# Attention over a key/value cache on one core: the instruction order of every engine written out in tables

## The chip, the core and the metric

The kernel runs on one core of a Trainium2 chip. The core has five engines with an instruction queue each: the tensor engine (PE in the profile, PEld for its weight loads), VectorE (DVE), ScalarE (ACT), GpSimd (POOL) and SyncE (SP, which issues all loads and stores here). Each works through its own queue in order; engines wait for one another on semaphores. The metric is the device time of one execution in microseconds (us), as the median of several runs.

## What is computed

Eight sequences of 112 queries are projected with `wq` into 32 heads of 192, attend to a cache of 512 keys and values per head, and are projected back with `wo`. All tensors are bf16.

```
B, Sq, D = 8, 112, 640;  H, Sk, Dh = 32, 512, 192
q = (x @ wq).reshape(B, Sq, H, Dh).transpose(0, 2, 1, 3)
scores = einsum("bhqd,bhkd->bhqk", q, k_cache) * Dh ** -0.5
p = softmax(scores)
o = einsum("bhqk,bhkd->bhqd", p, v_cache)
out = o.transpose(0, 2, 1, 3).reshape(B, Sq, H * Dh) @ wo
```

## The kernel before

**The work.** The 32 heads are taken in two halves of 16. A *tile* t (0 to 15) is one half of the heads of one sequence, and a *step* n (0 to 63) is four heads of a tile: n = 4t + s. Each instruction group has a name that the texts use:

- `X c`: transpose 128 rows of x on the tensor engine; `evX` copies the result out of PSUM.
- `KN`, `K`, `V`: loads of the cache. For tiles 0 and 1, K comes as it lies (`KN`), is transposed on the tensor engine (`K t u` in the tables, `KT` in the code) and copied out by `evK`. For the others one transposing load `K t` brings it. `V t 0` and `V t 8` load the values of eight heads each.
- `Qa`, `Qb (m, lp)`: the projection of two heads for two sequences, ten and five matmuls of 224 columns; `evQa`, `evQb` copy it out on ACT. `qc n` (DVE) copies parts of q to other partitions.
- `S n`: scores of a step, as `Sm` (two halves of four matmuls over all 128 rows of the array) and `St` (the rest of the head size, on 64 rows). They use PSUM banks 0 to 3.
- `smax` (DVE) scales scores into `s_sb` with a row minimum, `exp` (ACT) exponentiates and sums, `rc` and `norm` (DVE) divide. Four of each per step; `s_sb` has two places, so a `smax` waits for the `exp` two before it.
- `PT n j`: transposes of P on the tensor engine; `evPT n 0` copies the first half on ACT, `evPT n 1` the second on DVE. For steps 57 to 61 a transposing DMA `TD n` does it.
- `PV n`: P times V, as `PVt` (64 columns of the array) and `PVm`; `evPV` copies to `oT_sb` on ACT.
- `O (u, f, part)`: a part of the product with `wo` (matmuls of 224 columns) for unit u, that is eight heads of two sequences; `oacc u f` (DVE) adds it to `accT`. `O6`, `OL` and `OF` do the same for the last unit and turn the sums round for the output; `oout` (ACT) copies, `OUT` stores.

**The order.** Operations are declared with what they depend on (`Plan.add`), and `Plan.run` walks the list of each engine, waits for what an operation needs, and issues it. Semaphore values follow from the lists. So the lists are the program, and only they decide what stands behind what. A group that fills a PSUM bank waits for the copy that emptied it last (`fill`).

In the kernel before, the lists have three sources. Steps 0 to 8 are written out (`FRONT_PE`, `FRONT_ACT`, `FRONT_DVE`, and `FRONT_SP` for the first 34 loads). Steps 9 to 57 follow one rule, which puts on the tensor engine: the scores of step n, PV of step n-2, Q parts due, an O part, both transposes of step n-1, the rest of O and Q. ACT and DVE have rules of their own:

```
s_pe(n)                                      # scores of n
pv_pe(n - 2)
...                                          # Qa of the step, first part of O
pt_pe(n - 1)
...                                          # second part of O, Qb
act += [("exp", n, 0), ("exp", n, 1)] + [("evPV", n - 2)]
act += [("exp", n, 2)] + a_q + [("exp", n, 3)]
act += [("evPT", n - 1, 0)] + b_q
```

The last six steps are again lists (`TAIL` and two lists for ACT and DVE). The order of loads in the middle comes from a loop: `K t`, `V (t-1) 8`, a piece of a weight if one is due, `V t 0`. Q goes to banks 6 and 7, O to bank 7, PT and PV to banks 4 and 5 in these steps. A load waits on SP for its place to come free, and everything behind it in SP's list waits too: `K t` for the scores of step 4t - 5, `V` for the PV that last read its place, the second half of `wo` for the last O that reads the first.

Of the kernel before, what the change touches and what calls it, by code (L numbers as in the profile page):

```python
# [52 lines left out]
def build_mha_kernel(nc, x, k_cache, v_cache, wq, wo, out):  # L53
# [27 lines left out]
    with ExitStack() as es:  # L81
# [111 lines left out]
        def load_wq(half, lp, n=2):  # L193

            def emit(e):
                c0 = lp * 2 * DH
                g0 = half * HU * DH + c0
                return e.dma_start(wq_sb[:, :, c0:c0 + 2 * n * DH],
                                   wq[:, g0:g0 + 2 * n * DH].rearrange("(dc p) c -> p dc c", p=128))
            add("SP", ("WQ", half, lp), [("Qb", 3, lp + n - 1)] if half else [], emit, f"mWQ{lp}", 16)  # L200
            order["SP"].append(("WQ", half, lp))
            wq_piece.update({(half, lp + i): ("WQ", half, lp) for i in range(n)})

        def load_wo(half, u):
# [5 lines left out]
            old = [("O", 6 + u, 3, 1)] if half else [("KT", 1, HU - 1)]  # L210
# [31 lines left out]
        for b in range(B):  # L242
# [4 lines left out]
        FRONT_SP = [  # L247
            ("X", 0), ("WQ", 0, 0), ("KN", 0, 0, 4), ("WQ", 0, 2), ("KN", 0, 4, 4), ("WQ", 0, 4), ("KN", 0, 8, 8),
            ("WQ", 0, 6), ("V", 0, 0), ("X", 1), ("KN", 1, 0, 8), ("V", 0, 8), ("KN", 1, 8, 8), ("V", 1, 0),
            ("X", 2), ("K", 2, 0), ("V", 1, 8), ("WO", 0, 0), ("V", 2, 0), ("K", 3, 0), ("V", 2, 8), ("WO", 0, 1),  # L250
            ("V", 3, 0), ("K", 4, 0), ("V", 3, 8), ("V", 4, 0), ("K", 5, 0), ("V", 4, 8), ("WQ", 1, 0), ("V", 5, 0),
            ("K", 6, 0), ("V", 5, 8), ("WQ", 1, 2), ("V", 6, 0)]
        assert sorted(order["SP"][:len(FRONT_SP)]) == sorted(FRONT_SP)
        order["SP"][:len(FRONT_SP)] = FRONT_SP

        del order["SP"][-3:]
        order["SP"] += [
            ("TD", 57), ("V", 14, 8), ("TD", 58), ("OUT", 0), ("TD", 59), ("V", 15, 0), ("TD", 60), ("OUT", 1),
            ("TD", 61), ("OUT", 3), ("V", 15, 8), ("OUT", 4), ("OUT", 5), ("OUT", 2), ("OUT", 6), ("OUT", 7)]


        END = NN - 6
        NF = 9

        TAIL = [
            ("S", 58), ("OF", 3, 4), ("OF", 0, 5), ("O", 13, 1, 0, 7), ("O", 13, 1, 1, 7), ("O", 12, 2, 0, 6),
            ("OF", 1, 4), ("O", 12, 2, 1, 6), ("S", 59), ("OF", 2, 7), ("PV", 56, 4), ("O", 12, 3, 0, 6),
            ("O", 12, 3, 1, 6), ("O", 13, 0, 0, 7), ("O", 13, 0, 1, 7), ("S", 60), ("PV", 57, 4), ("O", 13, 3, 0, 7),
            ("O", 13, 3, 1, 7), ("O", 13, 2, 0, 6), ("O", 13, 2, 1, 6), ("PV", 58, 4), ("S", 61), ("PV", 59, 4),
            ("O6", 1, 0, 6), ("S", 62), ("O6", 1, 1, 6), ("O6", 0, 0, 7), ("OF", 5, 5), ("O6", 0, 1, 7),  # L270
            ("O6", 2, 0, 6), ("S", 63), ("PV", 60, 4), ("O6", 2, 1, 6), ("PV", 61, 0), ("OL", 0, 0),
            ("PT", 62, 0, 4), ("PT", 62, 1, 5), ("OL", 1, 0), ("OF", 4, 6), ("PT", 63, 0, 0), ("PV", 62, 4),
            ("PT", 63, 1, 1), ("OL", 0, 1), ("OL", 1, 1), ("PV", 63, 0), ("OL", 2, 0), ("OL", 2, 1), ("OL", 3, 0),
            ("OL", 3, 1), ("OF", 6, 4), ("OF", 7, 1)]
        end_bank = {tok[:-1]: tok[-1] for tok in TAIL if tok[0] not in ("S", "OL")}

# [163 lines left out]
        def transposes(n, j):  # L440
            bank = end_bank.get(("PT", n, j), 4 + j)
# [16 lines left out]
        def values(n):  # L458
# [3 lines left out]
            b0 = end_bank.get(("PV", n), 4)  # L462
# [45 lines left out]
        def o_bank(u, f):  # L508
            return end_bank.get(("O", u, f, 0), 7)
# [18 lines left out]
        def o_acc(u, f):  # L528
# [10 lines left out]
            deps = [("O", u, f, 1)] + ([("XT", B * SQ // 128 - 1)] if u == 0 else [])  # L539
# [13 lines left out]
        def o_six(g, part):  # L553

            def emit(e):
                for k in range(18, KB) if part else range(18):
                    w, o = wo_k(k)
                    for j, m in enumerate(SIX[g]):
                        mm = e.matmul(ps[:, end_bank["O6", g, 0], j * SQ:(j + 1) * SQ], w[:, m * 128:(m + 1) * 128], o[:, 0:SQ],
                                      start=(k == 0 and j == 0), stop=(k == KB - 1), skip_group_check=True)  # L560
                return mm
            add("PE", ("O6", g, part), [("evPV", step_of[NT - 2, 2 + part])], emit)

        def o_six_acc(g):
            m0, n = SIX[g][0], len(SIX[g])

            def emit(e):
                src = ps[:, end_bank["O6", g, 0], 0:n * SQ].rearrange("p (c s) -> p c s", c=n)
# [33 lines left out]
        def o_final(b):  # L602
            bp, bb = divmod(b, 2)
            bank = end_bank["OF", b]
# [14 lines left out]
        q_at = {n: [(1, n)] for n in range(4, 8)}  # L619
        for m in range(2, NM):  # L620
            for lp in range(LP):
                q_at[8 * m - (8 if (m, lp) < (3, 2) else 6) + lp] = [(m, lp)]
        o_at = {9: [(0, 0)], 10: [(0, 1)], 11: [(0, 2), (0, 3)], 13: [(1, 0)], 14: [(1, 1)], 15: [(1, 2), (1, 3)]}
        for u in range(2, 2 * NM - 2):
            for f in range(4):
                if 4 * u + 8 + f < END:
                    o_at[4 * u + 8 + f] = [(u, f)]
        whole = [o for n, os_ in o_at.items() for o in os_ if n not in q_at]
# [56 lines left out]
        def f_pe(b):  # L685
            fill(("OF", b), end_bank["OF", b], ("oout", b))
# [7 lines left out]
        def pt_pe(n):  # L694
            for j in range(2):
                fill(("PT", n, j), 4 + j, ("evPT", n, j))

        def pv_pe(n):
            for j in range(2):
                fill(("PVt", n), end_bank.get(("PV", n), 4) + j, ("evPV", n))  # L700
# [7 lines left out]
        def smaxes(n):  # L708
            return [("smax", n, i) for i in range(4)]

        FRONT_PE = [
            ("X", 1, 6, "DVE"), ("X", 0, 7, "DVE"), ("Z", 10), ("Qb", 0, 0, 3), ("Qa", 0, 1, 2), ("Qa", 0, 0, 4),
            ("K", 0, 1, 5, "ACT"), ("Qb", 0, 1, 3), ("K", 0, 2, 0, "ACT"), ("K", 0, 3, 5, "DVE"),
            ("K", 0, 0, 1, "ACT"), ("Qa", 0, 2, 7), ("S", 0), ("K", 0, 6, 5, "DVE"), ("K", 0, 5, 4, "DVE"),
            ("K", 0, 4, 6, "DVE"), ("Qa", 0, 3, 7), ("K", 0, 7, 0, "ACT"), ("Qb", 0, 3, 1), ("Qb", 0, 2, 7),
            ("Qb", 0, 4, 5), ("S", 1), ("Qa", 0, 5, 4), ("Qa", 0, 4, 7), ("Qb", 0, 5, 1), ("K", 0, 10, 0, "DVE"),
            ("K", 0, 11, 6, "DVE"), ("K", 0, 8, 3, "ACT"), ("K", 0, 9, 2, "ACT"), ("PT", 0, 1), ("Qb", 0, 6, 4),
            ("Qb", 0, 7, 1), ("K", 0, 13, 5, "DVE"), ("Qa", 0, 7, 3), ("PT", 0, 0), ("Qa", 0, 6, 7), ("S", 2),
            ("X", 2, 7, "DVE"), ("PV", 0), ("K", 0, 15, 6, "ACT"), ("X", 3, 0, "DVE"), ("K", 0, 12, 1, "ACT"),
            ("PT", 1, 0), ("PT", 1, 1), ("K", 0, 14, 2, "DVE"), ("Qa", 1, 0, 7), ("S", 3), ("PV", 1),  # L720
            ("Qb", 1, 1, 0), ("K", 1, 1, 7, "DVE"), ("Qa", 1, 1, 1), ("K", 1, 2, 2, "DVE"), ("PT", 2, 0),
            ("PT", 2, 1), ("K", 1, 5, 0, "ACT"), ("K", 1, 3, 6, "DVE"), ("Qa", 1, 3, 3), ("Qb", 1, 0, 5),
            ("K", 1, 0, 1, "ACT"), ("K", 1, 4, 6, "ACT"), ("K", 1, 6, 4, "DVE"), ("K", 1, 7, 5, "ACT"),
            ("Qa", 1, 2, 2), ("Qb", 1, 3, 7), ("S", 4), ("Qb", 1, 2, 6), ("PV", 2), ("K", 1, 10, 0, "DVE"),
            ("Qa", 1, 4, 1), ("Qb", 1, 4, 3), ("K", 1, 9, 2, "DVE"), ("K", 1, 8, 7, "DVE"), ("PT", 3, 0),
            ("PT", 3, 1), ("S", 5), ("PV", 3), ("Qa", 1, 5, 6), ("PT", 4, 0), ("K", 1, 11, 1, "DVE"), ("PT", 4, 1),
            ("K", 1, 12, 7, "ACT"), ("K", 1, 13, 6, "DVE"), ("Qb", 1, 5, 4), ("S", 6), ("PV", 4),
            ("K", 1, 15, 7, "DVE"), ("Qb", 1, 6, 0), ("Qa", 1, 6, 6), ("K", 1, 14, 2, "ACT"), ("PT", 5, 0),
            ("X", 4, 1, "DVE"), ("X", 6, 7, "DVE"), ("PT", 5, 1), ("S", 7), ("PV", 5), ("Qb", 1, 7, 0),
            ("Qa", 1, 7, 6), ("X", 5, 7, "DVE"), ("PT", 6, 0), ("S", 8), ("PT", 6, 1), ("Qb", 2, 0, 6), ("PV", 6),  # L730
            ("Qa", 2, 0, 7), ("PT", 7, 0), ("PT", 7, 1)]
        FRONT_ACT = [
            ("evQa", 0, 1), ("evQb", 0, 0), ("evQa", 0, 0), ("evK", 0, 1), ("evQb", 0, 1), ("evK", 0, 2),
            ("evK", 0, 0), ("evQa", 0, 2), ("exp", 0, 0), ("exp", 0, 1), ("evQa", 0, 3), ("exp", 0, 2),
            ("evQb", 0, 2), ("evQb", 0, 3), ("evK", 0, 7), ("exp", 0, 3), ("exp", 1, 0), ("exp", 1, 1),
            ("evQa", 0, 5), ("evQb", 0, 4), ("exp", 1, 3), ("evQb", 0, 5), ("evQa", 0, 4), ("evK", 0, 8),
            ("evQb", 0, 6), ("exp", 1, 2), ("evQb", 0, 7), ("evK", 0, 9), ("evQa", 0, 7), ("evQa", 0, 6),
# [203 lines left out]
```

## Time and profile before

| | us |
|---|---|
| median of 3 runs | 450.85 (450.34 to 454.32) |
| profiled execution | 452.17 |
| its span | 450.2 |
| tensor engine busy | 438.4 (97%) |
| DVE busy | 367.8 (82%) |
| ACT busy | 338.4 (75%) |
| mean granted clock of the tensor engine | 0.999 |
| HBM read | 73.50 MB |

The span runs from the first to the last instruction of the profiled execution; a little lies around it. Busy time counts an instruction from its start to its (for matmuls modelled) end. Times in the texts are counted from the start of the span.

### The profile page before, as it was taken

Reading aid. Unit: us, or ns where it says so; the run is one execution under the profiler, and the core shown is the slowest. Engines: PE = TensorE matmul, PEld = TensorE weight load, DVE = VectorE, ACT = ScalarE, POOL = GpSimd, SP = SyncE. Lnnn points to the kernel's source line nnn. Section 1 sums busy time; section 2 is a strip of 40 time slices with the busy share of each in tenths; the row PEclk is TensorE's granted clock in tenths of the full one; section 3 lists DMA queues with packets and bytes.
Section 4 is the critical chain, followed back from the end, with each engine's and each line's share of the span. In section 5 each row is a group of like instructions: output and inputs, shape, how many; then the busy total and the mean of one; then the engine's idle time right before and its main releaser. Section 6 shows DMA issues by size and latency. Waiting matters only on the chain.

```text
span 450.2 us, 15025 instructions
## 1 busy us (share of the span) xinstructions
PE 438.4 (97%) x6345; PEld 402.8 (89%) x6345; DVE 367.8 (82%) x1172; ACT 338.4 (75%) x787; POOL 0.7 (0%) x6
## 2 busy tenths in 40 slices
PE   8999999999999999999999999998999999999996
PEld 7799888998998899999999999997999989999986
DVE  1788789979888988898898888887798888889961
ACT  3688898868767877787687778767678777867683
POOL 0000000000000000000000000000000000000000
PEclk9999999999999999999999999999999999999999
DMA  8999999999999999999999999999999999999972
GB/s 296 373 376 359 238 302 245 250 328 277 261 275 279 315 240 352 232 336 258 274 290 232 287 229 341 261 261 363 227 306 187 276 220 217 273 244 269 223 193 67
DMA packets 232547, 121.94 MB, mean 271 GB/s; under 512 B 182560, under 2 KB 232480, under 8 KB 232480
## 3 DMA queue, kind: packets, MB, share of 16 engines
q1 hardware_dynamic: 232480, 120.99, 110.6%
q8 instruction: 50, 0.82, 0.7%
q14 instruction: 17, 0.14, 0.1%
HBM read 73.50 MB, written 1.15 MB: 166 GB/s over the span
## 4 chain that ended last, share of the span: by engine, by line
PE 85%; DMA 6%; DVE 4%; ACT 4%; issue 1%; SPq 0%; DVEq 0%; ACTq 0%
PE ps L329 18%; PE ps L520 17%; PE ps L486 11%; PE ps L447 10%; PE ps L397 7%; PE ps L475 6%; PE ps L384 6%; PE ps L386 6%; DMA wo_sb<-in_wo_dram 3%; DVE s_sb L412 3%; ACT p_sb L417 2%; PE ps L295 2%; DMA wq_sb<-p_sb 1%; DMA wq_sb<-in_wq_dram 1%; PE ps L583 1%
## 5 line engine op out<-in xcount | busy, mean ns | idle before, releaser
L417 ACT ACTIVATE p_sb<-s_sb,nmx 112x512 bf16<-112x512 f32 x256 | 183.2, 716 | 83.2 <-DVE s_sb L412 79.7
L412 DVE TENSOR_SCALAR_CACHE_REDUCE s_sb<-ps 112x512 f32<-112x512 f32 x256 | 167.5, 688 | 40.4 <-ACT p_sb L417 19.4
L329 PE MATMUL ps<-xT_sb,wq_sb 128*128 128x224 bf16 x960 | 111.1, 259 | 0.6 <-issue 0.4
L520 PE MATMUL ps<-oT_sb,wo_sb 128*128 128x224 bf16 x840 | 96.6, 259 | 1.8 <-DMA wo_sb<-in_wo_dram 1.8
L329 PEld LDWEIGHTS ps<-xT_sb,wq_sb 128*128 128x128 bf16 x960 | 88.6, 98 | 2.1 <-issue 0.9
L421 DVE TENSOR_SCALAR p_sb<-p_sb,rinv 112x512 bf16<-112x512 bf16 x256 | 79.3, 350 | 3.9
L520 PEld LDWEIGHTS ps<-oT_sb,wo_sb 128*128 128x128 bf16 x840 | 78.3, 98 | 2.1 <-DMA wo_sb<-in_wo_dram 2.1
L335 ACT ACTIVATE qr<-ps 128x448 bf16<-128x448 f32 (+1 forms) x112 | 49.1, 442 | 15.7 <-PE ps L329 15.6
L447 PE MATMUL ps<-ident,p_sb 112*128 112x112 bf16 x944 | 57.2, 213 | 1.2 <-ACT oT_sb L496 0.9
L453 ACT ACTIVATE pT_sb<-ps 128x896 bf16<-128x896 bf16 x59 | 53.5, 906 | 1.8 <-PE ps L447 1.1
L486 PE MATMUL ps<-pT_sb,vt 128*128 128x112 bf16 x912 | 54.8, 213 | 0.0
L447 PEld LDWEIGHTS ps<-ident,p_sb 112*128 112x128 bf16 x944 | 51.5, 98 | 3.4 <-ACT oT_sb L496 2.6
L486 PEld LDWEIGHTS ps<-pT_sb,vt 128*128 128x128 bf16 x912 | 45.8, 98 | 4.5
L417 ACT ACTIVATION_READ_ACCUMULATOR p_sb<-s_sb,nmx 112x1 f32 x256 | 49.0, 191 | 0.0
L496 ACT ACTIVATE oT_sb<-ps 128x672 bf16<-128x672 f32 x64 | 45.6, 712 | 3.8 <-PE ps L486 3.8
L453 DVE COPY pT_sb<-ps 128x896 bf16<-128x896 bf16 x59 | 36.4, 617 | 5.2 <-PE ps L447 5.2
L384 PE MATMUL ps<-kt,qh 128*112 128x256 bf16 x128 | 34.9, 273 | 0.0
L386 PE MATMUL ps<-kt,qh 128*112 128x256 bf16 x128 | 34.9, 272 | 0.0
L475 PEld LDWEIGHTS ps<-pT_sb,vt 128*64 128x64 bf16 x912 | 24.9, 109 | 10.9 <-issue 9.6
L475 PE MATMUL ps<-pT_sb,vt 128*64 128x112 bf16 x912 | 33.3, 216 | 0.8 <-issue 0.6
L399 PE MATMUL ps<-kt,qh 64*112 64x256 bf16 x128 | 34.0, 291 | 0.0
L384 PE MATMUL ps<-kt,qr 128*112 128x256 bf16 x112 | 30.7, 274 | 1.9 <-DVE qh L362 1.0
(68 smaller groups left out, 506.5 us busy)
## 6 DMA issues: line engine op xcount, KB each, us to landing
vt<-in_v_cache_dram SPq DMA_DIRECT2D x31, 1536.0 KB, 8.4
wq_sb<-in_wq_dram SPq DMA_DIRECT2D x8, 960.0 KB, 9.6
wo_sb<-in_wo_dram SPq DMA_DIRECT2D x4, 1920.0 KB, 13.0
wo_sb<-in_k_cache_dram SPq DMA_DIRECT2D x3, 1536.0 KB, 12.7
wo_sb<-in_k_cache_dram SPq DMA_DIRECT2D x2, 768.0 KB, 8.8
wq_sb<-in_v_cache_dram SPq DMA_DIRECT2D x1, 1536.0 KB, 8.0
out_dram<-xT_sb SPq DMA_DIRECT2D x8, 140.0 KB, 2.4
oT_sb<-in_x_dram SPq DMA_DIRECT2D x2, 320.0 KB, 8.9
```

Of the source, the lines that this page charges most:

```text
L329: mm = e.matmul(ps[:, bank, j * S2:(j + 1) * S2], wq_sb[:, dc, c0:c0 + 128], xT_sb[:, dc, bp * S2:(bp + 1) * S2], start=(dc == 0), stop=(d ...
L335: return e.activation(q_home(m, lp)[:, blocks[0]:blocks[0] + n, :], ps[:, bank, 0:n * S2].rearrange("p (c s) -> p c s", c=n), ACTF.Copy)
L384: e.matmul(ps[0:SQ, 2 * j, hs], ev, ktb[:, :, 0, cs(i)], start=(h == 0), stop=False, skip_group_check=True)
L386: mm = e.matmul(ps[0:SQ, 2 * j + 1, hs], od, ktb[:, :, 2, cs(i)], start=(h == 0), stop=False, skip_group_check=True)
L412: return e.tensor_scalar(s_sb[:, a, :].rearrange("p (e c) -> p e c", e=2), ps[0:SQ, 2 * j:2 * j + 2, h * 256:(h + 1) * 256], -scale, None, ...
L417: return e.activation(p_sb[:, k, :], s_sb[:, a, :], ACTF.Exp, bias=nmx[:, k:k + 1], scale=-1.0, accum_out=rsum[:, k:k + 1])
L421: return e.tensor_scalar(p_sb[:, k, :], p_sb[:, k, :], rinv[:, k:k + 1], None, op0=ALU.mult)
L447: mm = e.transpose(psb[:, bank, c:c + SQ], p_sb[:, (4 * n + 2 * j + h) % 8, q * 128:(q + 1) * 128], ident[0:SQ, 0:SQ])
L453: return e.activation(dst, src, ACTF.Copy) if j == 0 else e.tensor_copy(dst, src)
L475: mm = e.matmul(ps[64 * h:64 * h + 64, b0 + j, SQ:2 * SQ], vtb[:, h0 + 2 * j + h, d0:d0 + 64], pT(j, h, q), start=(q == 0), stop=(q == 3))
L486: mm = e.matmul(ps[:, b0 + j, 2 * h * SQ:(2 * h + 1) * SQ], vtb[:, h0 + 2 * j + h, d0:d0 + 128], pT(j, h, q), start=(q == 0), stop=(q == 3))
L520: mm = e.matmul(ps[:, o_bank(u, f), j * S2:(j + 1) * S2], wo_sb[:, KU * (u % 2) + k, m * 128:(m + 1) * 128], oT_sb[:, u % NO, k, :], start ...
```

## The change

All engines get one written table for the whole run: `ORDER_PE`, `ORDER_ACT`, `ORDER_DVE` and `ORDER_SP`. A token of `ORDER_PE` names the group and, where it has a choice, its PSUM bank (and for x and K transposes the engine of the copy). `FRONT_*`, `TAIL`, the rule, and the step tables `q_at` and `o_at` are gone. The number of matmuls, loads and stores is the same; seven copies of x and K move from DVE to ACT. `O` parts are cut at one place except for two of them (`whole`), as before. The dependences of `WQ` and `WO` name each reader, as the order no longer implies the last one.

```diff
-            add("SP", ("WQ", half, lp), [("Qb", 3, lp + n - 1)] if half else [], emit, f"mWQ{lp}", 16)
+            add("SP", ("WQ", half, lp), [("Q" + q, 3, lp + i) for i in range(n) for q in "ab"] if half else [], emit, f"mWQ{lp}", 16)
...
-            old = [("O", 6 + u, 3, 1)] if half else [("KT", 1, HU - 1)]
+            first, last = u * KB // 2 * D // 768, ((u + 1) * KB // 2 * D - 1) // 768
+            old = [("O", 6 + u, 3, 1)] if half else [("KT", t, v) for t in range(2) for v in range(first, last + 1)]
...
-        FRONT_SP = [
...
-        TAIL = [
...
+        ORDER_PE = [
+            ("Z", 10), ("X", 0, 7, "DVE"), ("X", 1, 4, "ACT"), ("Qb", 0, 0, 2), ("Qa", 0, 0, 3), ("Qa", 0, 1, 2),
+            ("K", 0, 0, 4, "ACT"), ("K", 0, 1, 3, "DVE"), ("Qb", 0, 1, 7), ("K", 0, 2, 6, "DVE"),
+            ("K", 0, 3, 4, "ACT"), ("K", 0, 4, 2, "ACT"), ("K", 0, 7, 7, "ACT"), ("K", 0, 5, 4, "DVE"),
+            ("K", 0, 6, 5, "DVE"), ("S", 0), ("Qa", 0, 2, 6), ("Qb", 0, 2, 7), ("Qb", 0, 3, 0), ("Qa", 0, 3, 1),
+            ("Qb", 0, 5, 7), ("Qa", 0, 5, 6), ("PT", 0, 0), ("S", 1), ("Qb", 0, 4, 5), ("X", 3, 4, "DVE"),
...
+            ("S", 16), ("Qa", 3, 1, 6),
+            ("O", 1, 3, 0, 7), ("O", 1, 3, 1, 7), ("PV", 14), ("S", 17), ("PT", 15, 0), ("PT", 15, 1),
...
+            ("S", 43), ("PV", 41), ("O", 8, 2, 1, 7), ("Qb", 6, 0, 0), ("Qa", 6, 1, 6), ("Qb", 6, 3, 5), ("S", 44),
+            ("PT", 42, 0), ("O", 8, 3, 0, 7), ("Qb", 6, 2, 6), ("Qa", 6, 2, 1), ("O", 8, 3, 1, 7), ("PT", 42, 1),
+            ("S", 45), ("PV", 42), ("Qb", 6, 5, 7), ("Qa", 6, 6, 6), ("O", 9, 0, 0, 7), ("O", 9, 0, 1, 7),
...
+        ORDER_DVE = [
...
+            ("smax", 9, 2), ("smax", 9, 3), ("rc", 9, 1), ("evPT", 8, 1), ("norm", 9, 2), ("smax", 10, 0), ("qc", 11),
+            ("smax", 10, 1), ("smax", 10, 2), ("rc", 9, 0), ("norm", 9, 0), ("oacc", 0, 1), ("smax", 10, 3),
...
+        ORDER_SP = [
+            ("X", 0), ("WQ", 0, 0), ("KN", 0, 0, 4), ("KN", 0, 4, 4), ("WQ", 0, 2), ("WQ", 0, 4), ("X", 1),
...
+            ("V", 3, 0), ("K", 4, 0), ("V", 3, 8), ("V", 4, 0), ("K", 5, 0), ("V", 4, 8), ("V", 5, 0), ("K", 6, 0),
+            ("WQ", 1, 0), ("V", 5, 8), ("V", 6, 0), ("K", 7, 0), ("V", 6, 8), ("WQ", 1, 2), ("WQ", 1, 4), ("V", 7, 0),
+            ("K", 8, 0), ("WQ", 1, 6), ("V", 7, 8), ("V", 8, 0), ("K", 9, 0), ("V", 8, 8), ("V", 9, 0), ("K", 10, 0),
...
-        for n in range(NF, END):
-            qs, os_ = q_at.get(n, []), o_at.get(n, [])
...
+        for kind, *a in ORDER_PE:
...
```

In the old loop of loads the weight piece stood behind `V (t-1) 8`; in the new table two of the `WQ` pieces stand ahead of it.

## The prediction

> **What bounds the kernel now.** I read the head of the page first, then the busy time by stage, then the waits, then the tensor engine's timeline, and last the loads. The head:
>
> ```profile
> span 450.2 us, 15025 instructions
> PE 438.4 (97%) x6345; PEld 402.8 (89%) x6345; DVE 367.8 (82%) x1172; ACT 338.4 (75%) x787; POOL 0.7 (0%) x6
> PEclk9999999999999999999999999999999999999999
> ```
>
> The tensor engine is busy in 97% of the span at full clock. A busy row includes the end of a matmul's pipeline, so I went on with distances between starts: 96 ns for a 224-column matmul (Q, O), 109 ns for the full scores, 49 ns for a transpose of P (PT) or a main matmul of P times V (PV). All its groups laid end to end at these distances take 427.3 us, the 45 ns pauses inside each of 64 scores another 2.9. From its first transpose to its last start the trace has 442.7. So about 12.5 us are waits; that is all that an order can win. By stage:
>
> ```profile
> core 0: us, PE busy (x) PEld busy (x) DVE busy (x) ACT busy (x) POOL busy (x), PEclk, DMA share, GB/s
> 0.00:25.00 25.00, 22.41 (x237) 19.25 (x238) 11.80 (x37) 14.06 (x32) 0.70 (x6) 1.00 0.97 338
> 50.00:75.00 25.00, 23.80 (x357) 20.82 (x357) 22.72 (x72) 21.21 (x50) 0.00 (x0) 1.00 1.09 291
> 150.00:200.00 50.00, 49.99 (x724) 46.22 (x721) 43.48 (x139) 38.37 (x92) 0.00 (x0) 1.00 1.17 285
> 300.00:350.00 50.00, 48.19 (x685) 44.56 (x683) 41.70 (x132) 37.28 (x88) 0.00 (x0) 1.00 1.16 271
> ```
>
> Between 150 and 200 us nothing is idle on it; the holes are in the first 75 us and at 300 to 350. What they wait for:
>
> ```profile
> PE ps L520 <- DMA wo_sb<-in_wo_dram: 1.8, 1, 1.8
> PE ps L384 <- DVE qh L362: 1.0, 1, 1.0
> PE ps L384 <- DVE s_sb L412: 0.9, 1, 0.9
> PEld ps L447 <- ACT oT_sb L496: 2.6, 6, 0.8
> ```
>
> Setting each group's first start against the distance from its predecessor gives where the waits are: 4.65 us between the first Q group (6.7 us) and the scores of step 9 (77.9 us); 4.2 in steps 9 to 57, of which 2.0 is the second half of wo (row one above) and 1.6 transposes of P behind a copy of oT (row four); 1.4 in the tail, 1.06 of it the last scores. The remaining 2.2 lie ahead of the first Q or in pauses inside groups that no row explains (0.55 us at 371 us); those I leave as they are.
>
> **The change, part by part.** The matmuls and loads are the same, in another order, so the sum has four terms. For the waits I laid the durations of this trace along the new tables: an instruction starts when its engine is free and when the last thing that it waits for has ended. Durations: exp 0.81 us (0.716 and 0.191, overlapping), smax 0.69, norm 0.35, qc 0.67, copies of P 0.91 on ACT and 0.61 on DVE, oacc 0.39 or 0.66; from a group's last matmul start to its copy 0.25 to 0.30; 0.12 more where a smax waits for two semaphores. The same addition over the old tables finds 4.2, 3.8 and 1.4 us of waits where the trace has 4.65, 4.2 and 1.4.
>
> *Scores and PV apart: +1.25 us.* The scores end in 64-row matmuls and PV begins with 64-column ones. Straight behind each other they look like the first three rows; with a group of five L608 between, like the others:
>
> ```profile
> 203.56 0.27 PE L397 MATMUL ps<-kt,qh 64*112 64x256 bf16 x1
> 203.57 0.27 PE L399 MATMUL ps<-kt,qr 64*112 64x256 bf16 x1
> 203.77 0.58 PE L475 MATMUL ps<-pT_sb,vt 128*64 128x112 bf16 x16
> ...
> 408.41 0.27 PE L399 MATMUL ps<-kt,qr 64*112 64x256 bf16 x1
> 408.61 0.49 PE L608 MATMUL ps<-ident,accT 128*112 128x128 bf16 x5
> 409.03 0.58 PE L475 MATMUL ps<-pT_sb,vt 128*64 128x112 bf16 x16
> ```
>
> The step to another array shape is 0.20 us in both; the second has a further one, 0.15 from L608's last start to L475 where its own distance is 0.056. So each separated pair costs 0.094 us, and 2 ns in the first step. Scores are followed directly by PV 56 times in the old order and 43 times in the new: 13 x 0.0965 = 1.25. Bounds: 0, if they fall into waits that exist anyway, and 13 x (0.213 - 0.049) = 2.1, if a whole matmul's latency were exposed. I take 1.25, the measured step.
>
> The Trainium skill, TensorEngine Tiling (Array Packing), Key Properties, says that changing the tiling mode drains the tensor engine; it speaks against this change. The trace agrees that there is a price, but shows 0.094 us for one more change; were each extra one a drain of the 0.213 us that a matmul lasts, this term would be 2.8 us.
>
> *Front, steps 0 to 8: -3.15 us.* The waits fall from 4.65 to 1.5. The largest old one, 1.18 us ahead of the scores of step 1 (row two), comes from K transpose (0,7): only three groups stood between it and those scores, and its copy on ACT came late. Now ten stand between, and 0.3 is left. The 0.61 and 0.67 us at K (1,14) and PV 6 go too. Seven copies move from DVE to ACT: three of K (0.55 there, 0.81 here) and four of x (0.49; not in the trace on ACT, between 0.49 and the 0.82 of a wider K copy; I take 0.70, the 640-wide output copy). ACT gains 5.2 us, DVE loses 3.6; ACT is free 18 of the first 75 us, which hides it; without that cover some 2 us. Ahead of the first Q nothing is won: ten idle matmuls stand before the x transposes instead of behind, but that Q waits for wq at 6.7 us either way. Bounds: -3.9 and -1.5.
>
> *Steps 9 to 57: +2.5 us.* O(9,0) is put behind the scores and PV of the next step; wo then lands 2 us ahead of it, and 2.0 goes. The 1.6 behind oT copies go too. Against that come 34 small waits, 6.7 us in sum. One worked out: the second pair of scores of step 11 needs smax(10,3); on DVE, smax(10,2), rc 0.16, norm 0.35, oacc(0,1) 0.66 and smax(10,3) 0.69 stand in a row and end at 89.30, while the tensor engine, through PV 8, O(0,1) and a Q, is there at 88.90: 0.45. By kind: scores behind smax 1.2, PV behind P copies 1.45, PT behind norm 1.1, O and Q behind the oacc or smax that empties their bank 1.5, V(3,8) 1.3. The last is where the front's lead runs into a load that has none. V(3,8) is queued behind K(4), whose issue held the queue 23.2 us; V(3,0) ahead of them waits for PV 9, which comes at the same time as before (94.9 us). It lands at 126.8; PV 14 is ready at 125.6. Bounds: half of the 6.7, if a wait makes room for the next, or half as much again, for waits on two semaphores.
>
> *Tail: -0.6 us.* The last scores' 1.06 us goes; four small waits come. Bounds -1.0 and 0.
>
> **Sum**: 1.25 - 3.15 + 2.5 - 0.6 = 0.0. The profiled execution took 452.2 us, its span of 450.2 and 1.9 around it; it lies 1.3 above the median of the runs. Both stay: 452.2 with profile, 450.9 us in the median.
>
> **The rivals.** *The small waits do not come* (445.2 us). If the copies run ahead far enough that only V(3,8) waits, the middle holds 1.0 instead of 6.7: 450.9 - 5.7. For it: most single waits are under 0.3 us, and DVE and ACT are free 6 and 12 of 50 us. Against: both stand in fixed order, and the addition was low, not high, on the old tables.
>
> *The lead is lost to the loads* (452.8 us). The new order is 3 us ahead at step 8; if K and V hand all of that back instead of 1.3, 1.9 is added. For it: the DMA share is 1.1 to 1.2 throughout, and K(4) lands as its scores are due.
>
> *The K loads run late* (456.3 us, slower). The K transpose load holds the queue for its issue, and the next V starts only behind it:
>
> ```profile
> 199.46 18.85 SPq L149 DMA_TRANSPOSE kt<-in_k_cache_dram  x1
> ```
>
> The fourteen run from 17.6 to 23.2 us, most when a wo load is beside. PV 29 now stands behind the scores of step 32, so V(8,0) and K(9) behind it start 3.5 us later: K(9) lands 1.2 us ahead of its scores where it had 6.3; V(5,8), now behind a wq load, has 0.9 (2.7 before), V(13,8) 0.4 (1.4). With 2 us more on every K the addition gives 5.4 more; it passes the 1% from 1.8 us each. Against: the same loads in the same neighbourhood took these times, with the DMA as full.
>
> **How the numbers follow.** Forecast 0.6, lead lost 0.2, no small waits 0.1, late K loads 0.1. The forecast's own range is the middle's bounds, 3.4 on each side: 447.5 to 454.3; the second rival lies within, and the others are the 2 in 10 left out. Faster or slower by over 1% (4.5 us, about what a measurement of this kernel can tell from no change) are the third and the last: 0.1 and 0.1; within 0.8.
>
> **What would show it.** Right: the scores of step 8 some 3 us earlier; no wait for wo over 0.5 us; PV behind V(3,8) near 126 us; issue waits of L475 and L397 together about 1.2 us longer; many waits of 0.1 to 0.4 on smax, P copies and norm in the middle. Wrong: a wait of over 2 us on K or V anywhere, under 3 us of waits in steps 9 to 57, or a lower PE clock.

## The result and the profile after

| | before | after |
|---|---|---|
| median, us | 451.9 (450.3 to 454.4, 18 runs) | 454.3 (453.2 to 455.1, 18 runs) |
| ratio after to before | | 1.0044, 95% interval 1.0028 to 1.0061 |
| profiled execution, us | 452.17 | 453.37 |
| its span, us | 450.2 | 451.6 |

The changed kernel is 0.4% slower: clear of the noise, but less than the 1% named in the prediction. The forecast was 450.9, no change; 454.3 is the very end of its range. The head of the page after (span, busy time by engine, granted clock of the tensor engine):

```profile
span 451.6 us, 15052 instructions
...
PE 442.3 (98%) x6345; PEld 401.3 (89%) x6345; DVE 358.2 (79%) x1165; ACT 350.3 (78%) x794; POOL 0.7 (0%) x6
...
PEclk9999999999999999999999999999999999999999
```

The tensor engine is busier (442.3 for 438.4 us) with the same 6345 instructions, and the span is longer all the same: a reader who takes busy time for progress is misled. The extra steps between array shapes count as busy (1.25 us, in the table below). So does most of a short wait, as it lies under the modelled end of the matmul before it: the waits and pauses of the table add up to 15.4 us before and 15.3 after, but the idle time (span less busy time) falls from 11.8 to 9.3. By stage of the kernel after (busy us of each engine with its instructions, clock, DMA share, GB/s):

```profile
core 0: us, PE busy (x) PEld busy (x) DVE busy (x) ACT busy (x) POOL busy (x), PEclk, DMA share, GB/s
0.00:25.00 25.00, 22.79 (x240) 20.09 (x241) 11.08 (x35) 15.63 (x34) 0.70 (x6) 1.00 0.97 340
...
50.00:75.00 25.00, 24.91 (x361) 22.32 (x360) 22.09 (x72) 24.17 (x55) 0.00 (x0) 1.00 1.14 301
...
150.00:200.00 50.00, 49.62 (x713) 45.53 (x711) 41.75 (x138) 39.44 (x90) 0.00 (x0) 1.00 1.15 285
...
300.00:350.00 50.00, 49.58 (x695) 45.13 (x694) 40.64 (x135) 37.28 (x87) 0.00 (x0) 1.00 1.16 283
```

The two holes of the old kernel are filled (50 to 75 us: 24.91 for 23.80; 300 to 350: 49.58 for 48.19). In exchange the stretches between 150 and 300 us, which had 0.1 us of holes in all (49.99 of 50 in the first), now have 0.4 in each 50 us. The waits (total, times, longest) show what they are:

```profile
PEld ps L780 <- issue: 6.8, 36, 0.4
...
PEld ps L689 <- DVE s_sb L717: 2.6, 8, 0.6
PEld ps L780 <- ACT p_sb L722: 2.3, 9, 0.6
PEld ps L780 <- ACT pT_sb L758: 2.2, 10, 0.5
PEld ps L752 <- DVE p_sb L726: 2.1, 6, 0.5
...
PE ps L634 <- ACT xT_sb L593: 0.9, 1, 0.9
...
PEld ps L825 <- DVE accT L843: 0.8, 3, 0.3
```

No row for wo is left. Instead there are many waits of a few tenths: scores (L689) behind smax (L717), PV (L780) behind copies of P (L758), transposes of P (L752) behind norm (L726), O (L825) behind oacc (L843).

From the first Q group to the last start, with every wait and pause counted (distance between starts, less the group's own distance):

| | before | after | difference | forecast |
|---|---|---|---|---|
| first Q starts (from span start) | 6.70 | 6.93 | +0.23 | 0 |
| work, with steps between shapes | 424.54 | 425.79 | +1.25 | +1.25 |
| waits up to the scores of step 9 | 5.51 | 2.91 | -2.60 | -3.15 |
| steps 9 to 57 | 7.91 | 10.53 | +2.62 | +2.5 |
| tail | 1.97 | 1.85 | -0.12 | -0.6 |
| sum | | | +1.38 | 0.0 |

The span differs by 1.4, so the table holds all of it.

### The profile page after: what moved, and what is told of

It is laid out like the page before. It is cut to its first block, busy times and chain, and to the rows that moved or that the text cites. A ratio compares the mean times of both kernels' runs of the same rounds, so it can differ in the third digit from the quotient of the medians.

```text
span 451.6 us, 15052 instructions
## 1 busy us (share of the span) xinstructions
PE 442.3 (98%) x6345; PEld 401.3 (89%) x6345; DVE 358.2 (79%) x1165; ACT 350.3 (78%) x794; POOL 0.7 (0%) x6
## 4 chain that ended last, share of the span: by engine, by line
PE 68%; DVE 7%; ACT 3%; issue 1%; DVEq 0%
PE ps L825 15%; PE ps L634 12%; PE ps L791 9%; PE ps L752 8%; PE ps L702 6%; PE ps L780 5%; PE ps L689 5%; PE ps L691 5%; DVE s_sb L717 4%; ACT p_sb L722 2%; DVE p_sb L726 1%; PE ps L864 1%; DVE qh L667 1%; PE ps L888 1%; DVE qh L666 1%
## 5 line engine op out<-in xcount | busy, mean ns | idle before, releaser
L717 DVE TENSOR_SCALAR_CACHE_REDUCE s_sb<-ps 112x512 f32<-112x512 f32 x256 | 171.7, 685 | 38.3 <-PE ps L704 14.3
L634 PE MATMUL ps<-xT_sb,wq_sb 128*128 128x224 bf16 x960 | 106.9, 259 | 1.1 <-ACT xT_sb L593 0.9
L825 PE MATMUL ps<-oT_sb,wo_sb 128*128 128x224 bf16 x840 | 94.1, 259 | 0.2
L634 PEld LDWEIGHTS ps<-xT_sb,wq_sb 128*128 128x128 bf16 x960 | 88.5, 98 | 3.7 <-DMA wq_sb<-in_wq_dram 1.2
L726 DVE TENSOR_SCALAR p_sb<-p_sb,rinv 112x512 bf16<-112x512 bf16 x256 | 82.4, 349 | 2.1
L825 PEld LDWEIGHTS ps<-oT_sb,wo_sb 128*128 128x128 bf16 x840 | 77.8, 98 | 1.6 <-DVE accT L843 0.8
L758 ACT ACTIVATE pT_sb<-ps 128x896 bf16<-128x896 bf16 x59 | 53.7, 911 | 10.4 <-PE ps L752 9.9
L752 PE MATMUL ps<-ident,p_sb 112*128 112x112 bf16 x944 | 60.7, 213 | 0.7 <-DVE p_sb L726 0.6
L640 ACT ACTIVATE qr<-ps 128x224 bf16<-128x224 f32 (+1 forms) x112 | 48.0, 444 | 11.5 <-PE ps L634 11.4
L752 PEld LDWEIGHTS ps<-ident,p_sb 112*128 112x128 bf16 x944 | 52.4, 98 | 4.9 <-DVE p_sb L726 2.1
L758 DVE COPY pT_sb<-ps 128x896 bf16<-128x896 bf16 x59 | 36.6, 620 | 13.0 <-PE ps L752 12.8
L780 PEld LDWEIGHTS ps<-pT_sb,vt 128*64 128x64 bf16 x912 | 25.1, 109 | 11.6 <-issue 5.6
L689 PE MATMUL ps<-kt,qh 128*112 128x256 bf16 x128 | 34.9, 272 | 0.0
L780 PE MATMUL ps<-pT_sb,vt 128*64 128x112 bf16 x912 | 33.3, 215 | 1.0 <-issue 0.4
L689 PE MATMUL ps<-kt,qr 128*112 128x256 bf16 x112 | 31.2, 278 | 0.5 <-DVE s_sb L717 0.4
## 6 DMA issues: line engine op xcount, KB each, us to landing
wq_sb<-in_wq_dram SPq DMA_DIRECT2D x8, 960.0 KB, 10.1
```

Of the source, the lines that this page charges most:

```text
L634: mm = e.matmul(ps[:, bank, j * S2:(j + 1) * S2], wq_sb[:, dc, c0:c0 + 128], xT_sb[:, dc, bp * S2:(bp + 1) * S2], start=(dc == 0), stop=(d ...
L640: return e.activation(q_home(m, lp)[:, blocks[0]:blocks[0] + n, :], ps[:, bank, 0:n * S2].rearrange("p (c s) -> p c s", c=n), ACTF.Copy)
L689: e.matmul(ps[0:SQ, 2 * j, hs], ev, ktb[:, :, 0, cs(i)], start=(h == 0), stop=False, skip_group_check=True)
L717: return e.tensor_scalar(s_sb[:, a, :].rearrange("p (e c) -> p e c", e=2), ps[0:SQ, 2 * j:2 * j + 2, h * 256:(h + 1) * 256], -scale, None, ...
L726: return e.tensor_scalar(p_sb[:, k, :], p_sb[:, k, :], rinv[:, k:k + 1], None, op0=ALU.mult)
L752: mm = e.transpose(psb[:, bank, c:c + SQ], p_sb[:, (4 * n + 2 * j + h) % 8, q * 128:(q + 1) * 128], ident[0:SQ, 0:SQ])
```

## The experiments

Each kernel was run beside the kernel before, and its ratio is to that kernel, measured at the same time. My theory: the changed kernel loses in the middle, because DVE and ACT end just behind the tensor engine there. Rivals: the steps between array shapes, or the loads.

**Norm on 2 of 512 columns, in both kernels.** The same line in each (L421 before, L726 after); it leaves the softmax undivided in the other 510 columns:

```diff
-  return e.tensor_scalar(p_sb[:, k, :], p_sb[:, k, :], rinv[:, k:k + 1], None, op0=ALU.mult)
+  return e.tensor_scalar(p_sb[:, k, 0:2], p_sb[:, k, 0:2], rinv[:, k:k + 1], None, op0=ALU.mult)
```

> The order before, with each norm on 2 of its 512 columns instead of all (it leaves the softmax undivided almost everywhere): DVE gets 0.28 us shorter in each of 256 places. Theory (the changed order keeps the DVE and ACT chains too close to the tensor engine; the old order has slack there): almost nothing here, waits 10.5 to 9.6, so about 0.8 us faster, 451. Rival (the time sits in loads or in the tensor engine's own steps): 0 here and 0 in the changed order.

> The changed order, with each norm on 2 of its 512 columns (it leaves the softmax undivided almost everywhere). Theory: the waits of the middle on smax, norm and P copies mostly go, some 4.5 to 5 us; 449.5, faster than the order before by 2 us though it parts 13 more pairs. Rival (loads, or array switches alone): within 1 us of 454.3, the same as the same edit does to the order before.

Before: 450.9 us, ratio 0.9997 (0.997 to 1.0024). After: 447.9 us, 0.9915 (0.9889 to 0.9941), 6.4 below the changed kernel's own median. About 30 us are taken off DVE (a norm falls from 0.35 to 0.23 us, less than expected). The old order gains nothing that its interval can tell from no change, and the new one overtakes it. Half of the old order's 12 executions with the short norm ran at a granted clock of 0.996 or less; the six at 0.999 and above have a median of 450.4 us, about 1 us below the kernel before at such a clock. The chain of work that ended last, by engine, first of the kernel after and then of the same with the short norm:

```profile
PE 68%; DVE 7%; ACT 3%; issue 1%; DVEq 0%
```

```profile
PE 72%; DMA 3%; DVE 3%; ACT 1%; issue 0%; SPq 0%; DVEq 0%
```

DVE's share falls from 7% to 3%, and a load of wo comes in instead. The waits in steps 9 to 57 fall from 10.53 to 6.92 us in the new order, and from 7.91 to about 7.0 in the old one: with the shorter norm the 2.6 us by which the new middle was worse are gone. So the middle's loss is DVE's, as the theory had it. The changed kernel with the short norm has 43 pairs of scores and PV and the loads of the changed kernel, so neither rival alone keeps that one slow.

**Seventeen pairs parted, in the kernel before.** In 17 steps (10, 13, 14, 15 and on to 57) PV stands behind the step's Q group:

```diff
-            pv_pe(n - 2)
+            if n not in APART:
+                pv_pe(n - 2)
...
+                if n in APART:
+                    pv_pe(n - 2)
```

> The order before, with the Qa group put between scores and PV in 17 of the steps 10 to 57, where PV can be later by 0.96 us without a wait. Theory: each parted pair costs 0.096 us of tensor engine time, 1.64 in all; waits fall by about 0.5 as they are filled, so 1.1 us slower, about 453.0; in the profile 17 more groups with the 0.20 and 0.15 us steps around them. Rival (the steps vanish in waits): 0, 451.9.

451.5 us, ratio 0.9993 (0.9975 to 1.0011): no cost in the time, where my theory had 453.0 and the rival 451.9. The cost is in the trace all the same. From the timeline of the tensor engine (start, us, line):

```profile
120.75 0.35 PE L329 MATMUL ps<-xT_sb,wq_sb 128*128 128x224 bf16 x2
121.03 0.58 PE L475 MATMUL ps<-pT_sb,vt 128*64 128x112 bf16 x16
```

The second L329 matmul starts 0.096 behind the first, at 120.85; PV follows 0.19 later instead of 0.096. All 17 steps into PV are 0.189, and the step out of the scores stays at 0.20. That is 17 x 0.0965 = 1.64 us more work, as priced. But the waits in steps 9 to 57 fall by 1.33. The largest part is the wait for wo, 1.97 before and 0.90 here. That load lands at 313.1 us where it landed at 312.55: more work ahead of it costs nothing up to its landing. Another 0.98 is the tail's, where nothing was changed: with the old tail the last scores wait 1.0 to 1.4 us in some executions and under 0.2 in others. So a price can be right and not show, if a load behind it comes when it comes.

**O(9,0) alone one step later, in the kernel before.**

```diff
+        del o_at[44]
+        o_at[45] = [(9, 0), (9, 1)]
```

> The order before, with O(9,0) moved from step 44 to step 45 beside O(9,1), as late as the changed order has it. Theory: the 2.0 us wait for the second half of wo goes and 1.4 to 2.0 us are won, 450.2. Rival (the loads' chain sets the pace): the wait comes back at the next K or V load and the time stays at 451.9.

450.2 us, ratio 0.9969 (0.995 to 0.9988): a gain of 1.4 of the 1.9 us. (By the rule of the middle the edit also puts step 44's `Qb` straight behind its `Qa`.) In its profiled execution, which with 452.1 us is the second longest of twelve and no faster than that of before, the wait went to the next load, in the waits list:

```profile
PE ps L475 <- ACT p_sb L417: 1.6, 1, 1.6
```

The row names an exp that had long ended. What came last is V (11,8): it lands at 336.43, PV 46 starts at 336.57 us. It was issued behind the K load, whose issue held the queue until 327.90:

```profile
305.08 22.78 SPq L149 DMA_TRANSPOSE kt<-in_k_cache_dram  x1
327.90 2.67 SPq L164 DMA_DIRECT2D vt<-in_v_cache_dram  x2
```

Theory and rival are both partly right: the median falls as the theory had it, and in this execution the next load takes most of the gain back (another 1.4 us stand at the tail's last scores).

**The new front with the old rest.** Tables of the changed kernel up to the scores of step 8, the old order behind.

> The changed kernel's tables up to the scores of step 8, and the old order from the scores of step 9 on (the old pairs of scores and PV behind step 9, the old tail, the old loads behind the first 34). It tells the front's term apart from the middle's. My theory: the front's gain is real (2.5 us of waits fewer in the trace of the changed kernel), and most of it arrives, since the old middle keeps its order: the addition of durations gives a last start 0.7 to 1.2 us ahead of the old kernel's, because some 1 us comes back at the seam (scores of step 9, transposes of step 8) and the wo wait of 2 us stays. So about 450.5 us beside 451.7, ratio 0.997. Rival 1: the middle hands nothing back: 449, ratio 0.994. Rival 2: the lead runs into the loads, whose place in the middle is not earlier: 451.7 or more, ratio 1.000 or above, with longer waits for wo or V than the old kernel has.

453.0 us, ratio 1.0035 (1.0008 to 1.0062): slower, and my theory fell. The median needs care: five of the twelve executions had a granted clock of 0.995 or 0.996 and took 454.2 to 456.6 us; the seven at 0.998 and above have a median of 451.7, no better than the kernel before and no worse. The profiled one is of the second kind (451.69 us, full clock), so its trace shows why the front's gain did not arrive, not what slowed the five. Counted from the first Q, the scores of step 8 come 2.2 us earlier than before, those of step 12 0.55 us later. The stage of 75 to 100 us, before and here:

```profile
75.00:100.00 25.00, 25.00 (x362) 23.18 (x358) 21.69 (x72) 19.69 (x46) 0.00 (x0) 1.00 1.22 254
```

```profile
75.00:100.00 25.00, 22.68 (x331) 19.77 (x330) 20.68 (x66) 18.47 (x45) 0.00 (x0) 1.00 1.14 297
```

The tensor engine stands 2.3 of 25 us. Its waits there are for copies: 0.94 at the scores of step 9 (ACT's copy of Q), 0.75, 0.47 and 0.50 at the transposes of steps 8 to 10. The first comes from the seam: `Qb (1,7)`, which the changed kernel has between the two transposes of step 8, stands straight ahead of the scores of step 9 here and fills a bank that they need. From the scores of step 9 to those of step 12 the waits exceed the old kernel's by 3.3 us, more than the 2.6 that the front had saved. The front puts the tensor engine ahead; DVE and ACT, which also have seven copies rearranged, are not ahead with it, and the old lists behind step 9 leave no room to catch up. How much of this belongs to the seam alone is not shown. Rival 2 had the time right but not the place: not V or wo, the two copying engines. The wo wait was there as before (2.07 at 313.9).

**Searched tables.** If waits between engines set the time, an order that avoids them should beat both.

> The same operations under other tables: entries of all four lists were moved one at a time, from the old kernel's order, so that the durations of the traces laid along the tables end early, and also with 0.2 us added to every handover between engines. With the handovers of the traces the addition ends at 437.3 us where it gives the old order 446.0 and the changed one 446.2; with 0.2 us more on each it ends at 442.9 where it gives them 476 and 485. 51 scores are followed directly by PV. My theory (waits between engines set the time, loads do not): 442 to 446 us in the median, ratio 0.98 to 0.987, PE waits of under 6 us in all. Rival: the loads are the bound once the waits are gone, as the wo wait came back as a wait for V in one trace: not under 447.5 us, ratio 0.99 or above, with waits for V or K of over 1 us in several places.

> As the kernel before this one, but started from the changed kernel's tables and their dependences: 437.1 us with the traces' handovers, 444.8 with 0.2 us more on each, 41 scores followed directly by PV. My theory: 443 to 447 us, ratio 0.98 to 0.99, up to 1 us behind its sister for the ten pairs fewer (0.0965 us each). Rival 1: the pairs cost more than the 0.0965 us: over 2 us behind its sister. Rival 2, the loads: not under 447.5 us.

474.0 us (1.0488, 1.0463 to 1.0513) and 482.7 us (1.0678, 1.0656 to 1.0701), 20 us and more slower than the old kernel. My theory fell by some 30 and 37 us; the rivals had the cause, loads, but nothing near the size. The searches had also moved loads, and the addition gave each load at the start a fixed service time whatever stood around it. In the first, wq's first piece had gone behind another piece, a load of K and one of V, and the first Q stood (in the second, 14.0 us for the same piece):

```profile
PE ps L639 <- DMA wq_sb<-in_wq_dram: 9.1, 1, 9.1
```

Long waits cost more than themselves: after the 3.48 us wait that ends at 212.5 us the clock falls. Its stretches (us, length, busy times, granted clock PEclk):

```profile
206.00:208.50 2.50, 2.50 (x36) 2.32 (x33) 1.94 (x7) 2.05 (x5) 0.00 (x0) 1.00 1.06 374
208.50:212.30 3.80, 0.61 (x9) 0.36 (x8) 3.21 (x12) 1.64 (x5) 0.00 (x0) 1.00 1.06 377
212.30:214.00 1.70, 1.48 (x33) 1.43 (x34) 0.78 (x3) 0.00 (x0) 0.00 (x0) 0.93 1.06 374
214.00:216.00 2.00, 2.00 (x13) 1.56 (x12) 0.00 (x0) 0.74 (x2) 0.00 (x0) 0.50 1.06 372
```

**The same search with the list of loads kept**: the changed kernel's list and its tables as a start, and the old list and the old order.

> The two searched orders fell because their loads were moved. Here the list of loads is that of the changed kernel, entry for entry; only the tables of the tensor engine, DVE and ACT are searched, with up to 1.5 us more on every load and 0 to 0.2 us more on every handover. 39 scores are followed directly by PV, four fewer than in the changed kernel. With the traces' handovers and loads the addition ends at 437.6 us where it gives the changed order 444.2 (its trace: 448.0), with 0.2 us more on each handover at 446.5 (484.6 for the changed one). My theory (the order of the three engines sets the waits between them, and a lead is kept where DVE and ACT have it too and the loads have place): waits of 4 to 7 us instead of 12, so 446 to 449 us, ratio 0.986 to 0.993, though the pairs cost 0.4 us more. Rival 1: the loads are the floor: ratio 0.995 or above, with waits of over 1 us for V, wo or the transposing loads of P at the end. Rival 2: handovers vary more than the addition allows: many small waits again, ratio 1.0 or above.

> The same search with the old kernel's list of loads, started from the old order: 438.7 us by the addition (444.6 for the old order, whose trace has 446.6), 448.1 with 0.2 us more on each handover (476 for the old one), 42 pairs. My theory: 447 to 450 us, ratio 0.988 to 0.996, about 1 us behind its sister for the later loads. Rival 1, loads: ratio 0.997 or above with a wait at wo's second half, V (11,8) or the last P transposes. Rival 2 as for the sister.

The first: 447.9 us, ratio 0.9909 (0.9884 to 0.9935), faster than both kernels. The second: 451.6 us, 0.9991 (0.9966 to 1.0015), no gain: there the rival of the loads came true. The first one's waits, in full for scores and transposes of P behind DVE:

```profile
PEld ps L689 <- DVE s_sb L717: 1.5, 1, 1.5
...
PE ps L825 <- DMA wo_sb<-in_wo_dram: 1.2, 1, 1.2
...
PEld ps L752 <- ACT oT_sb L801: 0.4, 2, 0.2
```

The L689 row had 8 waits in the changed kernel and has one here, in the tail; the row of L752 behind norm is gone. Steps 9 to 57 hold 5.25 us instead of 10.53 (four waits above 0.05 instead of 30), though 39 pairs are left instead of 43. One edit in detail, the wait of the prediction's worked example. The changed kernel, DVE and tensor engine (start, us):

```profile
88.79 0.17 DVE L734 RECIPROCAL rinv<-rsum 112x2 f32<-112x2 f32 x1
88.99 0.35 DVE L726 TENSOR_SCALAR p_sb<-p_sb,rinv 112x512 bf16<-112x512 bf16 x1
89.26 0.62 DVE L841 COPY accT<-ps 128x448 f32<-128x448 f32 x1
...
89.80 0.68 DVE L717 TENSOR_SCALAR_CACHE_REDUCE s_sb<-ps 112x512 f32<-112x512 f32 x1
...
90.54 0.32 PE L689 MATMUL ps<-kt,accT 128*112 128x256 bf16 x1 [0.39 <-DVE s_sb L717]
```

And with the searched tables:

```profile
87.06 0.68 DVE L717 TENSOR_SCALAR_CACHE_REDUCE s_sb<-ps 112x512 f32<-112x512 f32 x1
...
87.68 0.35 DVE L726 TENSOR_SCALAR p_sb<-p_sb,rinv 112x512 bf16<-112x512 bf16 x1
...
88.13 0.62 DVE L841 COPY accT<-ps 128x448 f32<-128x448 f32 x1
...
88.37 0.27 PE L689 MATMUL ps<-kt,accT 128*112 128x256 bf16 x1
```

`smax(10,3)` stands ahead of norm and `oacc` instead of behind, and the scores of step 11 run through. Beside the 1.5 at the last scores, what is left is mostly loads: 1.35 for wo at 311.6, 0.81 and 0.77 for wq in the front. The sister with the old loads stood at them all over (wq 1.43 at 231.5, V 0.92 at 150.2 and 1.35 at 337.0), and held 9.23 us in steps 9 to 57.

**Lists of loads exchanged.**

> The old order of the tensor engine, DVE and ACT with the changed kernel's list of loads. My theory: an order and its list of loads belong together, and the loads alone bring nothing: the addition gives 2.6 to 3.1 us more than with the old loads (some loads of x and wq at the start come behind others, and wo's second half comes no earlier), so 452.5 to 455 us, ratio 1.002 to 1.008. Rival: the new list of loads is simply the better one (it held no engine in the kernel of 447.9 us but at wo): 450 us or less, ratio under 0.997.

> The changed kernel's order of the three engines with the old list of loads up to the last step's V. My theory: the front's new order needs its x and K loads where they now stand, and the tensor engine's lead runs into wq and K: the addition gives 8 us more than with its own loads, so 460 us, ratio 1.015 to 1.022, with waits for x, K (0) and V of several us. Rival: the loads are not near the bound, and the many small waits set the time: 454 to 456 us, ratio 1.003 to 1.009.

> The searched order of 447.9 us with the old list of loads up to the last step's V. My theory: 7 to 10 us more by the addition (438 to 445 or 448), most of it in the front and at K (4), V (3,8) and K (9); since that order stood at loads in few places, some of it falls into them: 454 to 457 us, ratio 1.005 to 1.012. Rival: the old list does as well, and the gain over its sister with the old loads (451.6) was the order of the engines: 449 us or less, ratio under 0.995.

458.0 us (1.012, 1.0084 to 1.0156), 465.4 us (1.0298, 1.0262 to 1.0334) and 461.8 us (1.020, 1.0165 to 1.0235). The directions were as the addition had them, the sizes all larger. The changed order with the old loads, its waits:

```profile
PE ps L586 <- DMA oT_sb<-in_x_dram: 5.6, 1, 5.6
...
PEld ps L689 <- DVE s_sb L717: 2.6, 8, 0.6
PE ps L634 <- DMA wq_sb<-in_wq_dram: 2.4, 1, 2.4
...
PE ps L600 <- DMA wo_sb<-in_k_cache_dram: 2.2, 1, 2.2
...
PEld ps L752 <- DVE p_sb L726: 2.1, 6, 0.5
```

The second piece of x is issued at 14.46 us instead of 5.70, and the front, which now transposes it early, waits. The rows of L689 and L752 are the changed kernel's, digit for digit: though the start moved by 9 us, the small waits of the middle are the same. So they belong to the order, not to an execution. The searched order with the old loads loses 13.9 us, 10.1 of it ahead of step 9 (11.72 us of waits for 1.61). The old order with the new loads loses 5 us there. Neither list of loads is better by itself.

## Why the prediction was right, point by point

*The steps between shapes, +1.25*: right in size. It was measured at 0.093 us for each of 17 steps, and the reading of the Trainium skill's rule (TensorEngine Tiling (Array Packing), Key Properties) as a full drain of 0.213 us each is not what the trace shows. What the step left out is that such a price can vanish where a load follows, as in the experiment; the changed kernel no longer waits for wo, and the table has the price in full in its work.

*Front, -3.15*: -2.60. The kind was right, every large old wait went; 0.42 was left at PT 1 behind norm and 0.27 at the scores of step 1. It also said that ahead of the first Q nothing changes. There 0.23 is lost, since that Q waits for a copy of x that now runs on ACT, the L634 row above. That is one execution: with the same tables the first Q came at 6.73 us (behind wq, short norm), 6.92 and, with the old rest, 7.60. It follows the first rise of the granted clock (at 4.40, 4.84 and 6.24 us), as the ten idle matmuls, 0.21 us apart before that rise and 0.11 behind it, now stand ahead of the transposes of x; in the old order it came at 6.7 to 7.0 whether the clock rose at 3.9 or 6.7. The front put ahead of the old order shows what else it needs: the tensor engine lost the lead again within three steps where the lists behind step 9 were not those that go with it.

*Steps 9 to 57, +2.5*: +2.62 with every pause counted; by the prediction's own count of waits 6.6 us where it had 6.7. The worked example came at 90.54 with 0.55 instead of 0.45. One part was wrong: V (3,8) did not hold PV 14. K (4) held the queue 17.7 us, not 23.2, V (3,8) landed at 122.3, and PV 14 came 4.8 us later. The 1.3 us booked for it came elsewhere. By kind, said and measured: scores 1.2 and 1.8, PV behind P copies 1.45 and 1.5, PT 1.1 and 1.7, O and Q 1.5 and 1.6, V (3,8) 1.3 and none. That the sum held although this part was wrong is luck.

*Tail, -0.6*: -0.12. The mis-sized term is the old one: the 1.06 us at the last scores is a matter of the execution, as the kernels with the same tail show (under 0.1 in three of them, 1.0 to 1.4 in three). In the new tail the PV that needs V (15,8) stands 0.50, until 439.74; that load lands at 439.40, last of what it needs.

*Sum*: +1.38 for 0.0. Front and tail were over-booked by 0.55 and 0.48, the first Q by 0.23, the middle by 0.12. The profiled executions are 1.2 us apart, the medians 2.4: that of before was 0.3 slower than its median, that of after 0.9 faster, and the sum was made from one execution each. So the kinds of wait were foreseen; that a change of 0.4% still lay inside the stated range, at its last tenth of a microsecond, is in part luck.

*The rivals*: no small waits would have been 445.2; they came. The lead was not lost to the loads. By span time it was 2.0 us at step 8 and 2.5 at step 16, but such dates also move with the groups that now stand ahead of a step. By waits alone it was 2.6 us at step 9 and still 2.4 at step 24, then went into the small waits: 1.4 at step 32, 0.6 at step 40, none at step 58. K loads were not late: K (9) had 3.5 us in hand, V (13,8) 3.3.

*The marks*: scores of step 8 came 2.0 us earlier, not 3. The issue rows of L475 and L397 were to grow by 1.2: L397's (now L702) stayed at 11.4, L475's (now L780) fell from 10.3 to 6.8, for a PV that is parted from its scores waits under the name of a copy. The step's price showed in the timeline, not in that row: it was a badly chosen mark.

## What to carry to other kernels

A handwritten order for several engines is one object together with its list of loads: the other kernel's list of loads cost 1.2, 2.4 and 3.1% here, against the same order with its own list (458.0 for 451.9 us, 465.4 for 454.3, 461.8 for 447.9), though each list was good in its own kernel. Where DVE and ACT are about 80% busy beside a full tensor engine, look first for copies that stand behind a longer piece of work on DVE or ACT while the next group waits for them: reordering these three tables, with the loads kept, gave 1.3% over the changed kernel (0.9909 against 1.0044). And a term of a sum that rests on a single wait in one execution needs a second execution before it is booked.

## What the runs showed of the hardware

The transposing load of K held its queue for 16.4 to 21.9 us in the changed kernel, 17.6 to 23.2 before. The second half of wo landed between 311.4 and 313.9 us in nine kernels with quite different orders ahead of it (before, after, both short norms, the parted pairs, O moved, the front alone, both searched ones with their loads kept); where the front itself had stood for loads it came later (318.2 in the old order with the new loads), and where a search had moved the loads, at 299.8 and 331.8. That fits the old kernel gaining so little from a lighter DVE: up to there it can't run ahead of that load. SP's queue itself is not full: between 39 and 312 us it holds no load for 55 us before, 72 after and 47 in the faster searched kernel. (A row of its timeline that merges two loads hides the pause between them.)

The granted clock: after the wait of 3.48 us shown above it was 0.50 until 217.2 us, and ten matmuls of Q took 0.82 us more. The same happened after waits of 2.21 and 2.67 us in that kernel and after one of 1.92 in the old order with the new loads, but not after 2.07, 2.39, 2.59 and 2.94 in others. All of 3.2 us and more were followed by it. So the length of a wait does not decide it. In every trace the clock changes at multiples of 3.41 us from its first rise. On this grid each stretch at full clock in which the tensor engine was busy 1.43 us or less was followed by a drop, and none with 1.49 us or more; between, one with 1.47 was and two with 1.44 and 1.46 were not (busy times are modelled). First the stretch with the 3.48 us wait and the one after it, then those of the kernel before around its wait for wo:

```profile
210.36:213.77 3.41, 1.25 (x31) 1.20 (x32) 2.67 (x10) 0.23 (x2) 0.00 (x0) 1.00 1.06 375
213.77:217.18 3.41, 3.41 (x23) 2.74 (x21) 0.00 (x0) 1.92 (x4) 0.00 (x0) 0.50 1.06 368
...
309.37:312.79 3.42, 1.61 (x22) 1.36 (x19) 2.94 (x11) 3.42 (x9) 0.00 (x0) 1.00 1.07 371
312.79:316.20 3.41, 3.41 (x45) 3.23 (x45) 1.73 (x6) 1.56 (x4) 0.00 (x0) 1.00 1.30 245
```

The wait of 1.92 us fell into one such stretch, that of 2.94 us into two. A drop cost 1.5 to 1.7 us where the tensor engine had work through the stretch. The Trainium skill, TensorE: Matmul & The Clock Gate, Part 1, gives half rate after at least one idle window of about 3.4 us, free-running. The grid of the traces agrees; but a window need not be idle here, as 1.47 us of work in it did not prevent the drop.

Both profiled executions of this case show a full clock, yet the kernel before does not always: 15 of its 74 executions beside the experiments had 0.996 or less (452.4 to 455.8 us), the other 59 0.998 and above (450.0 to 453.5, median 451.3). All 18 of the changed kernel had 0.998 and above; its longest wait is 1.05 us, ahead of the first Q. Which wait lowers the clock in those 15 is not shown; in the trace its wait for wo, with 1.61 us of work in the stretch, comes nearest. Beside the 451.3 of a clock without a drop the changed kernel's 454.3 is 3 us slower, not 2.4.
